# K pairs one place later, their tokens spread over three w2 pairs, phi of the third segment's K moved there, and the mixing product in one step

## The chip, the cores and the metric

The kernel runs on one core of a Trainium2 chip. The metric is the device time of one execution in microseconds; the profile's span (first to last instruction) is about 1.7 to 2 us shorter.

Names: TensorE (PE, weight loads PEld), VectorE (DVE), ScalarE (ACT), GpSimd (POOL), SyncE (SP). SyncE does nothing here but issue DMAs, in program order, waiting for each one's semaphores.

## The reference, cut to what matters

```python
xn = layernorm(x)                                  # x: 2048 tokens x 1024
# B: token MLP with weights w1 (2048 x 3584) and w2 (3584 x 2048)
# A: attention, 32 heads of 32, in 4 segments of 512 tokens, with a memory M, z over segments
q, k, v = xn @ wq, xn @ wk, xn @ wv
phi = lambda t: where(t > 0, t + 1, exp(t))
for s in range(4):
    a_dot = softmax(qs @ ks.T * scale + mask) @ vs
    a_mem = (phi(qs) @ M) / (phi(qs) @ z + 1e-6)
    outs.append(g * a_mem + (1 - g) * a_dot)       # the "mixing"
    M, z = M + phi(ks).T @ vs, z + sum(phi(ks))
return x + concat(outs) @ wo + B(layernorm(xn))
```

phi of K is needed for three segments only: the memory after the fourth is not used.

## The kernel before: the parts that the change and the argument touch

The MLP's products are done by a seven-product scheme (Winograd's form of Strassen's): a *pair* of 128-column blocks takes 7 products, in the order 1, 6, 5, 7, 2, 4, 3. A w2 pair has 7 x 14 matmuls, and there are 8 of them, here counted 0 to 7. Between them stand 4 *K pairs* (7 x 4 matmuls each), which compute K of segments 3 and 4 and store it in DRAM. After the w2 stage comes attention: 32 *units* (8 per segment, counted 0 to 31); a unit's time runs from its first exponential on ScalarE to the next unit's.

```python
    N_KP, K_FIRST = N_GRP // 2, 3                  # order: w2 0 1 2, K, 3, K, 4, K, 5, K, 6 7

    def k_prepare(self, i, p):                     # after product p of w2 pair i
        n = self.ORDER.index(p)
        if i < 2:                                  # 8 blocks of tokens (128 each) of segments 3, 4
            c = 8 + 4 * i
            if n in (2, 3, 4, 5):
                m = n - 2
                self.xn_scale(c + m, F16)          # VectorE
                ...                                # DMA transpose xnK <- xs, on SyncE
            if n < 4:
                self.xn_load(c + n)                # two buffers xs: waits for the transpose that reads it
        g = i - self.K_FIRST + 1
        if g == 0 and n < 4:                       # pair 2: the four differences of the K scheme
            self.differences(self.kB, self.R_kB, self.kD, self.R_kD, (n + 1,))
        ...
    def after2(self, pair, p):                     # cut
        elif p == 4:
            finish("Y", 1, 0, t1)
            self.put_out(...)
            if i + 2 < self.N_W2:
                self.load_w2(i + 2)                # 1.79 MB on SyncE's queue
        ...
        self.k_prepare(i, p)
        if i >= self.N_W2 - 2:                     # pairs 6 and 7: two of attention's first tokens each
            c = 2 * (i - self.N_W2 + 2)
            if p in (1, 6):
                self.xn_load(c + (p == 6))
            elif p in (5, 7):
                self.xn_scale(c + (p == 7))
                self.xn_transpose(c + (p == 7))
        if i == self.N_W2 - 1:
            self.before_attention(p)               # after 1: wq, wk; after 6: wv (2 MB); after 2: wo (2 MB)
```

In a unit of attention, TensorE's matmuls are cut into stretches; at certain stops one entry of a list of *side work* is taken, which is mostly VectorE's:

```python
            self.jobs.extend(self.unit_jobs(u))    # unit_jobs also issues the k load of unit u + 2
            if xn:
                self.xn_load(c)                    # a token of the next segment
            ...
                steps = self.combine(u - 1)        # [scales, products(0), products(1), add]
                self.side.append(steps.pop(0))
            if N_GRP <= u:
                self.side.append(lambda u=u: self.phi_q(u))
            if u:
                self.side.extend(steps)
            if u + 1 < N_UNIT:
                self.side.append(lambda u=u: (self.phi_k(u + 1), self.k_transpose(u + 1)))
            if xn:
                self.side.append(lambda c=c: (self.xn_scale(c), self.xn_transpose(c)))
```

## Time and profile before

| | us |
|---|---|
| time, median of 3 | 676.55 (675.97 to 676.81) |
| span of the profiled run | 673.8 |
| w2 pair 1 / 2 / the undisturbed ones | 22.7 / 30.3 / 21.15 |
| first K pair / the other three | 7.9 / 6.24 |
| units 16 to 22, even / odd | 9.78 / 7.1 to 7.6 |
| unit 24 (no phi of K) | 8.89 |

From the page of the kernel before, TensorE's line of section 1 (busy us, share, count) and the granted clock in 40 slices:

```profile
PE 643.2 (95%) x4559; PEld 301.9 (45%) x4610; DVE 449.6 (67%) x853; ACT 281.1 (42%) x305; POOL 147.3 (22%) x181
...
PEclk9999999999999979999999999999999999999999
```

TensorE is nearly always busy, so only its gaps and its one clock dip can be won. The table of windows of the kernel before, cut at w2 pairs 1 and 2, the first K pair, pair 3, pair 7 and units 16 to 23 (length, then busy time and count for each engine, granted clock, DMA share, GB/s):

```profile
core 0: us, PE busy (x) PEld busy (x) DVE busy (x) ACT busy (x) POOL busy (x), PEclk, DMA share, GB/s
201.04:223.72 22.68, 21.32 (x100) 9.50 (x99) 9.07 (x12) 0.60 (x1) 4.23 (x3) 1.00 0.84 212
223.72:253.97 30.25, 23.14 (x99) 9.90 (x98) 16.20 (x20) 0.60 (x1) 4.23 (x3) 0.89 0.51 129
253.97:261.85 7.88, 6.31 (x29) 2.57 (x28) 6.30 (x10) 1.19 (x2) 0.00 (x0) 1.00 0.95 245
261.85:283.00 21.15, 21.15 (x99) 9.60 (x98) 8.98 (x14) 0.60 (x1) 4.23 (x3) 1.00 0.33 105
365.17:386.54 21.37, 21.32 (x99) 9.66 (x99) 7.18 (x14) 2.11 (x3) 4.60 (x6) 1.00 0.99 252
530.10:597.80 67.70, 61.75 (x694) 30.95 (x705) 63.83 (x133) 53.32 (x52) 26.96 (x33) 1.00 0.59 141
```

Pair 2 has the same 98 matmuls as pair 3 and takes 9.1 us more, with a clock of 0.89. In the last line VectorE is busy 63.8 of 67.7 us, TensorE 61.8: VectorE is the bound there. The timeline of the kernel before shows what happened in pair 2 (start, duration, engine, what; in brackets the idle time before it and what ended it):

```profile
227.60 0.45 SPq L220 DMA_DIRECT2D w2s<-in_B_w_dram  x1
228.71 6.70 SPq L220 DMA_TRANSPOSE xnK<-xs  x1
...
238.17 1.23 DVE L664 TENSOR_TENSOR kD<-xnK,xnK 128x2048 f16<-128x2048 f16 x1 [7.84 <-issue]
...
240.06 5.01 PE L198 MATMUL ps_all<-g,sum 128*128 128x512 f16 x14 [7.11 <-DVE part L690]
```

A token's transpose normally keeps SyncE 1.23 us and lands about 3 us after its issue. This one stood behind a w2 load of 1.79 MB: 6.70 us of issue, landed at 237.9. VectorE stood before the first K difference until then, and TensorE 7.1 us behind VectorE; then 14 matmuls took 5.0 us instead of 3.2, at half clock. In attention the chain of work that ended last runs through VectorE (start, us, what; the view leaves the shortest pieces out):

```profile
536.09 0.69 DVE pqT L1183
536.79 1.05 DVE prod L1413
537.86 1.01 DVE prod L1413
539.24 0.73 DVE mtmp L1181
540.00 1.00 DVE mtmp L1183
```

### The profile page before, as it was taken

Reading aid. Unit: us, or ns where it says so; the run is one execution under the profiler, and the core shown is the slowest. Engines: PE = TensorE matmul, PEld = TensorE weight load, DVE = VectorE, ACT = ScalarE, POOL = GpSimd, SP = SyncE. Lnnn points to the kernel's source line nnn. Section 1 sums busy time; section 2 is a strip of 40 time slices with the busy share of each in tenths; the row PEclk is TensorE's granted clock in tenths of the full one; section 3 lists DMA queues with packets and bytes.
Section 4 is the critical chain, followed back from the end, with each engine's and each line's share of the span. In section 5 each row is a group of like instructions: output and inputs, shape, how many; then the busy total and the mean of one; then the engine's idle time right before and its main releaser. Section 6 shows DMA issues by size and latency. Waiting matters only on the chain.

```text
span 673.8 us, 11152 instructions
## 1 busy us (share of the span) xinstructions
PE 643.2 (95%) x4559; PEld 301.9 (45%) x4610; DVE 449.6 (67%) x853; ACT 281.1 (42%) x305; POOL 147.3 (22%) x181
## 2 busy tenths in 40 slices
PE   8999999999999879999999999999999998999987
PEld 3444444444444333444444444455444444444444
DVE  6965766656652565627445326756998999997895
ACT  7532322313200001000011047778767877788860
POOL 2500000000020120201202203433233433444340
PEclk9999999999999979999999999999999999999999
DMA  8704332422959828256183966755665467444425
GB/s 309 192 1 125 85 102 63 125 64 63 241 156 252 195 62 234 67 167 182 52 248 93 275 184 165 155 120 117 144 147 103 126 163 166 112 104 111 117 59 133
DMA packets 188972, 93.96 MB, mean 139 GB/s; under 512 B 108536, under 2 KB 175096, under 8 KB 188920
## 3 DMA queue, kind: packets, MB, share of 16 engines
q1 hardware_dynamic: 188776, 93.20, 53.7%
q8 instruction: 36, 0.59, 0.4%
q14 instruction: 16, 0.13, 0.1%
q10 hardware_dynamic: 144, 0.03, 0.0%
HBM read 69.23 MB, written 10.49 MB: 118 GB/s over the span
## 4 chain that ended last, share of the span: by engine, by line
PE 48%; DVE 12%; issue 3%; ACT 1%; DMA 1%; DVEq 0%
PE ps_all L198 48%; DVE prod L1413 3%; DVE ost L1366 2%; DVE pqT L1183 1%; ACT pT L1315 1%; DVE mtmp L1181 1%; DVE fin L1258 1%; DVE mtmp L1183 1%; DVE srec L1408 1%; DMA oT<-o_s 1%; DVE fin L1559 1%; DVE MZbf L1376 0%; DVE srec L1409 0%; DVE xs L1087 0%; DVE sum L649 0%
## 5 line engine op out<-in xcount | busy, mean ns | idle before, releaser
L1315 ACT ACTIVATE pT<-ps_all 128x2048 bf16<-128x2048 f32 x80 | 150.1, 1876 | 49.9 <-PE ps_all L198 49.7
L1319 POOL TENSOR_SCALAR_AFFINE_SELECT pT<-pT 128x512 bf16<-128x512 bf16 x128 | 98.2, 784 | 175.9 <-ACT pT L1315 175.9
L690 DVE TENSOR_TENSOR part<-ps_all,part 128x512 f32<-128x512 f32 x84 | 58.0, 691 | 109.7 <-PE ps_all L198 108.9
L1025 POOL TENSOR_TENSOR part<-part,stg 128x512 f32<-128x512 f32 x24 | 33.2, 1409 | 301.6 <-DVE part L690 301.6
L695 ACT ACTIVATE part<-ps_all 128x512 f32<-128x512 f32 x24 | 14.3, 597 | 168.1 <-PE ps_all L198 168.1
L746 ACT ACTIVATE g<-part,b1c 128x512 f16<-128x512 f32 x36 | 26.0, 722 | 98.7 <-DVE part L690 98.7
L198 PE MATMUL ps_all<-wv,xnT 128*128 128x512 bf16 x241 | 63.3, 380 | 1.4 <-DVE kT L1213 0.8
L198 PE MATMUL ps_all<-wo,oT 128*128 128x512 bf16 (+2 forms) x257 | 62.7, 366 | 1.2 <-DMA oT<-o_s 0.3
L198 PE MATMUL ps_all<-xnT,wq 128*128 128x512 bf16 x241 | 60.6, 379 | 1.3 <-issue 1.1
L198 PE MATMUL ps_all<-g,sum 128*128 128x512 f16 x224 | 52.8, 389 | 7.1 <-DVE part L690 7.1
L198 PEld LDWEIGHTS ps_all<-vA,pT 128*128 128x128 bf16 x1280 | 45.0, 96 | 27.9 <-DVE ost L1366 13.4
L1366 DVE CAST ost<-ps_all 128x396 bf16<-128x396 f32 (+2 forms) x96 | 43.4, 472 | 18.3 <-PE ps_all L198 17.7
L198 PE MATMUL ps_all<-vA,pT 128*128 128x33 bf16 x1280 | 48.6, 178 | 6.0 <-DVE ost L1366 6.0
L198 PE MATMUL ps_all<-g,w2s 128*128 128x512 f16 x224 | 51.0, 379 | 0.0
L198 PE MATMUL ps_all<-gT,sum 128*128 128x512 f16 x224 | 49.7, 379 | 0.0
L1413 DVE TENSOR_TENSOR prod<-ost,srec 128x512 bf16<-128x512 bf16 x48 | 45.9, 956 | 0.8
L198 PE MATMUL ps_all<-h,sum 128*128 128x512 f16 x192 | 45.2, 379 | 0.0
L198 PE MATMUL ps_all<-h,w1s 128*128 128x512 f16 x192 | 44.9, 379 | 0.0
L198 PE MATMUL ps_all<-hT,sum 128*128 128x512 f16 x192 | 43.6, 379 | 0.0
L198 PEld LDWEIGHTS ps_all<-g,sum 128*128 128x128 f16 x224 | 22.2, 100 | 35.2 <-DVE part L690 7.6
L198 PE MATMUL ps_all<-qT,kT 32*128 32x384 bf16 (+3 forms) x512 | 31.7, 301 | 3.8 <-ACT pT L1315 1.9
L198 PEld LDWEIGHTS ps_all<-xnT,wq 128*128 128x128 bf16 x256 | 22.9, 97 | 27.3 <-issue 4.4
(115 smaller groups left out, 850.6 us busy)
## 6 DMA issues: line engine op xcount, KB each, us to landing
w2s<-in_B_w_dram SPq DMA_DIRECT2D x8, 1792.0 KB, 8.7
w1s<-in_B_w_dram SPq DMA_DIRECT2D x12, 1024.0 KB, 5.4
wq<-in_A_wq_dram SPq DMA_DIRECT2D x32, 256.0 KB, 3.2
xs<-in_A_x_dram SPq DMA_DIRECT2D x24, 256.0 KB, 3.5
stg<-in_A_x_dram SPq DMA_DIRECT2D x16, 256.0 KB, 4.1
out_dram<-stg SPq DMA_DIRECT2D x16, 256.0 KB, 3.1
wk<-in_A_wk_dram SPq DMA_DIRECT2D x16, 256.0 KB, 3.5
fin<-out_dram SPq DMA_DIRECT2D x16, 256.0 KB, 3.4
```

The costliest lines, as they stand in the source:

```text
L198: ins = self.nc.tensor.matmul(*args, **kwargs)
L690: self.fw.op("dve", lambda e: e.tensor_tensor(self.tmp[dst][:], self.bank(b), self.tmp[src][:], op=ALU.add), reads=[self.R_bank[b], self.R ...
L695: self.fw.op("act", lambda e: e.activation(self.tmp[dst][:], self.bank(b), ACT.Copy), reads=[self.R_bank[b]], writes=[self.R_tmp[dst]])
L746: self.fw.op("act", lambda e: e.activation(self.gB[f % 2][half][:, f // 2, :], src, ACT.Gelu_apprx_tanh, bias=self.b1c[:, f:f + 1], scale= ...
L1025: fw.op("pool", lambda e: e.tensor_tensor(self.tmp[t][:], self.tmp[t][:], self.stg[k][:, 512 * half:512 * half + 512], op=ALU.add), reads= ...
L1181: fw.op("dve", lambda e: e.tensor_scalar(mt[:], et[:], 1.0, None, op0=ALU.min), reads=[R_et], writes=[self.R_mtmp[k]])
L1183: fw.op("dve", lambda e: e.scalar_tensor_tensor(dst, src, 1.0, mt[:], op0=ALU.add, op1=ALU.max), reads=[R_src, self.R_mtmp[k]], writes=[R_ ...
L1258: self.fw.op("dve", lambda e: e.tensor_tensor(dst, self.bank(b), dst.bitcast(F16), op=ALU.add), reads=[self.R_bank[b], R], writes=[R])
L1315: fw.op("act", lambda e: e.activation(dst, src, ACT.Exp, scale=SCALE), reads=self.R_bank[0:4], writes=[R[v % 2][kb] for v, kb, _ in blocks ...
L1319: fw.op("pool", lambda e: e.affine_select(d, d, pattern=[[0, 4], [1, P]], compare_op=ALU.is_ge, fill=0.0, base=0, channel_multiplier=-1), ...
L1366: fw.op("dve", lambda e: e.tensor_copy(dst, src), reads=[self.R_bank[b]], writes=[self.R_ost[o][part]])
L1413: fw.op("dve", lambda e: e.tensor_tensor(self.prod[:, n, :], ost[:, n, 0:D_HEAD], rec[:, n].unsqueeze(2).to_broadcast([P, 16, D_HEAD]), op ...
```

## The change: its intent, and the diff

Three intents: the eight tokens of the K pairs get more time each, and the K differences a pair more (K pairs one place later, tokens over pairs 0 to 2); VectorE loses work in units 16 to 22 (phi of the third segment's K is computed in the K pairs, stored in DRAM and read back by a transposing DMA); and it runs one product of 1024 columns instead of two of 512. K pairs later also means that the memory of attention's first tokens is free only in pair 7, so all four tokens go there.

```diff
-    N_KP, K_FIRST = N_GRP // 2, 3
+    N_KP, K_FIRST = N_GRP // 2, 4
@@ after_k: put(acc, row, col, t)
-            fw.dma(self.k_d[v], dst[:], reads=[R], writes=[self.R_kd[v]], is_output=True)
+            if (row, col) in ((0, 1), (1, 0)):        # both columns of a row in one store
+                ...
+            if col == 0:
+                n = t1 if row else t3
+                e, R_e = self.tmp[n][:].bitcast(BF16)[:, 0:SEG_L], self.R_tmp[n]
+                fw.op("act", lambda q: q.activation(e, dst, ACT.Exp), ...)
+                fw.op("dve", lambda q: q.tensor_scalar(e, e, 1.0, None, op0=ALU.min), ...)
+                fw.op("dve", lambda q: q.scalar_tensor_tensor(e, dst, 1.0, e, op0=ALU.add, op1=ALU.max), ...)
+                fw.dma(self.pk_d[v], e, reads=[R_e], writes=[self.R_pkd[v]], is_output=True)
@@ k_prepare(i, p)
-        n = self.ORDER.index(p)
-        if i < 2: ...
+        n = 7 * i + self.ORDER.index(p)
+        if n % 2 == 0 and 2 <= n // 2 < 10:           # a token at every second product
+            m = n // 2 - 2
+            c = 8 + m
+            self.xn_scale(c, F16)
+            self.fw.dma(self.xnK[m // 4][...], self.xs[c % 2][:].bitcast(F16), ..., transpose=True, own=True)
+        if n % 2 == 0 and n // 2 < 8:
+            self.xn_load(8 + n // 2)
+        n %= 7
         ...
+        if i == self.N_W2 - 1:                        # attention's first four tokens, all in pair 7
+            if 1 <= n < 5:
+                self.xn_scale(n - 1)
+                self.xn_transpose(n - 1)
+            if n < 3:
+                for c in ((0, 1), (2,), (3,))[n]:
+                    self.xn_load(c)
@@ after2
-        if i >= self.N_W2 - 2: ...                    # two tokens in pair 6, two in pair 7
@@ k_transpose(u)
+        if 0 <= v < N_GRP:
+            self.fw.dma(self.pk[j][:], self.pk_d[v], reads=[self.R_pkd[v]], writes=[self.R_pk[j]], transpose=True)
@@ combine(u)
-        return [scales, lambda: products(0), lambda: products(1), add]
+        return [scales, products, add]
```

More of the change, by code (lines that the diff above doesn't have):

```diff
@@ L903, in kout @@
         def kout(w, k):
-            t, (r,) = w.take(f"kout{k}", [P, SEG_L], BF16)
+            t, r = w.take(f"kout{k}", [P, 2, SEG_L], BF16, 2)
             self.kout.append(t)
@@ L908, in alloc_w2_rest @@
         kout(w, 0)
+        w = _Walk(self.mem, self.B_AT + self.K_AT, self.B_AT + self.FREE_AT)
         kout(w, 1)
-        w = _Walk(self.mem, self.B_AT + self.K_AT, self.B_AT + self.FREE_AT)
-        kout(w, 2)
-        kout(w, 3)
         self.xs, self.R_xs = [], []
@@ L936, in alloc_w2_rest @@
         self.R_kd = [Res(f"kd{u}") for u in range(N_UNIT // 2)]
+        self.pk_d = self.nc.dram_tensor("pk_part", (N_GRP, P, SEG_L), BF16).ap()
+        self.R_pkd = [Res(f"pkd{u}") for u in range(N_GRP)]
         self.load_wkp(0)
@@ L966, in put @@
         def put(acc, row, col, t):
-            n, b = 2 * row + col, pair.bank[acc]
-            dst, R = self.kout[n], self.R_kout[n]
+            b = pair.bank[acc]
+            dst, R = self.kout[row][:, col, :], self.R_kout[row][col]
             if t is None:
-                fw.op("act", lambda e: e.activation(dst[:], self.bank(b), ACT.Copy), reads=[self.R_bank[b]], writes=[R])
+                fw.op("act", lambda e: e.activation(dst, self.bank(b), ACT.Copy), reads=[self.R_bank[b]], writes=[R])
             else:
-                fw.op("dve", lambda e: e.tensor_tensor(dst[:], self.bank(b), self.tmp[t][:], op=ALU.add),
+                fw.op("dve", lambda e: e.tensor_tensor(dst, self.bank(b), self.tmp[t][:], op=ALU.add),
                       reads=[self.R_bank[b], self.R_tmp[t]], writes=[R])
             v = N_GRP * col + 2 * g + row
-            fw.dma(self.k_d[v], dst[:], reads=[R], writes=[self.R_kd[v]], is_output=True)
+            if (row, col) in ((0, 1), (1, 0)):
+                v = 2 * g + row
+                fw.dma(self.k_d.rearrange("(c v) p t -> v p c t", c=2)[v], self.kout[row][:], reads=self.R_kout[row],
+                       writes=[self.R_kd[v], self.R_kd[v + N_GRP]], is_output=True)
+            if col == 0:
+                n = t1 if row else t3
+                e, R_e = self.tmp[n][:].bitcast(BF16)[:, 0:SEG_L], self.R_tmp[n]
+                fw.op("act", lambda q: q.activation(e, dst, ACT.Exp), reads=[R], writes=[R_e])
+                fw.op("dve", lambda q: q.tensor_scalar(e, e, 1.0, None, op0=ALU.min), reads=[R_e], writes=[R_e])
+                fw.op("dve", lambda q: q.scalar_tensor_tensor(e, dst, 1.0, e, op0=ALU.add, op1=ALU.max),
+                      reads=[R, R_e], writes=[R_e])
+                fw.dma(self.pk_d[v], e, reads=[R_e], writes=[self.R_pkd[v]], is_output=True)
         if p == 1:
@@ L995, in k_prepare @@
     def k_prepare(self, i, p):
-        n = self.ORDER.index(p)
-        if i < 2:
-            c = 8 + 4 * i
-            if n in (2, 3, 4, 5):
-                m = n - 2
-                self.xn_scale(c + m, F16)
-                s, cc = (c + m) // 4, m
-                x = self.xs[m % 2]
-                self.fw.dma(self.xnK[s - 2][:, :, cc * P:(cc + 1) * P], x[:].bitcast(F16), reads=[self.R_xs[m % 2]],
-                            writes=[self.R_xnK[s - 2][cc]], transpose=True, own=True)
-            if n < 4:
-                self.xn_load(c + n)
+        n = 7 * i + self.ORDER.index(p)
[3 more added lines that the diff above has]
+            self.xn_scale(c, F16)
+            self.fw.dma(self.xnK[m // 4][:, :, (m % 4) * P:(m % 4 + 1) * P], self.xs[c % 2][:].bitcast(F16),
+                        reads=[self.R_xs[c % 2]], writes=[self.R_xnK[m // 4][m % 4]], transpose=True, own=True)
+        if n % 2 == 0 and n // 2 < 8:
+            self.xn_load(8 + n // 2)
+        n %= 7
         g = i - self.K_FIRST + 1
@@ L1068, in after2 @@
         self.k_prepare(i, p)
-        if i >= self.N_W2 - 2:
-            c = 2 * (i - self.N_W2 + 2)
-            if p in (1, 6):
-                self.xn_load(c + (p == 6))
-            elif p in (5, 7):
-                self.xn_scale(c + (p == 7))
-                self.xn_transpose(c + (p == 7))
         if i == self.N_W2 - 1:
@@ L1191, in phi_k @@
     def phi_k(self, u):
-        if u // N_GRP < N_SEG - 1:
+        if u < N_UNIT // 2:
             k = u % 3
@@ L1196, in k_transpose @@
     def k_transpose(self, u):
-        if u // N_GRP < N_SEG - 1:
-            j = u % 2
+        j, v = u % 2, u - N_UNIT // 2
+        if 0 <= v < N_GRP:
+            self.fw.dma(self.pk[j][:], self.pk_d[v], reads=[self.R_pkd[v]], writes=[self.R_pk[j]], transpose=True)
+        elif v < 0:
             self.fw.dma(self.pk[j][:], self.mtmp[1][:], reads=[self.R_mtmp[1]], writes=[self.R_pk[j]], transpose=True)
@@ L1409, in scales, with products @@
             fw.op("dve", lambda e: e.tensor_tensor(rv, rv, g8, op=ALU.mult), reads=[R_rec, self.R_gate], writes=[R_rec])
-        def products(half):
-            n = slice(16 * half, 16 * half + 16)
-            fw.op("dve", lambda e: e.tensor_tensor(self.prod[:, n, :], ost[:, n, 0:D_HEAD],
-                                                   rec[:, n].unsqueeze(2).to_broadcast([P, 16, D_HEAD]), op=ALU.mult),
-                  reads=R_ost + [R_rec, self.R_prod], writes=[self.R_prod])
+        def products():
+            fw.op("dve", lambda e: e.tensor_tensor(self.prod[:], ost[:, :, 0:D_HEAD],
+                                                   rec.unsqueeze(2).to_broadcast([P, 32, D_HEAD]), op=ALU.mult),
+                  reads=R_ost + [R_rec], writes=[self.R_prod])
         def add():
@@ L1524, in attention @@
             self.dense(100)
-            if N_UNIT // 2 <= u + 2 < 3 * N_GRP:
-                self.exps.append((1, self.kT[(u + 2) % 3], self.R_kT[(u + 2) % 3], u + 2))
         while self.side:
```

## The prediction

> **What bounds it now.** TensorE is busy 95% of the 673.8 us span, so only its gaps can be won. From the timeline and the table of windows:
> - w2 stage, 180-386 us. A pair takes 21.1 us undisturbed. Pair 1 took 22.7 us (a 1.35 us gap), pair 2 30.2 us: TensorE idle 7.1 us at 233-240, then granted clock 0.53 (240-244 us), so 14 matmuls took 5.0 us, not 3.2. The first K pair took 7.9 us, the second 6.2. Loss about 12 us. Cause: the fourth and eighth token transposes were issued about 1 us after a 1.79 MB w2 load and held the SyncE queue 7.2 and 6.7 us; VectorE waited for the tokens (7.8 us before the first K difference), TensorE for VectorE.
> - Attention. Units 16-22 have VectorE idle 0.3-0.7 us each and TensorE idle 0.5-1.0 us; the even ones take 9.78 us against 8.9 in unit 24, which lacks phi of K. VectorE bounds there (63.1 us busy of 530-597). Loss about 5.5 us; units 10, 11, 26, 30 and the end have about 2-3 us more.
>
> **What the change does.**
> 1. Tokens at every second product over three pairs, differences a whole pair later. Two transposes still follow a w2 load, but there are 12 us per token instead of about 3. Walking the queue by hand leaves about 1 us of stall. Gain 11 us.
> 2. Phi of segment 3's K leaves attention: 8 x (VectorE 0.29 to 0.72 + 0.69 to 1.0 us, ScalarE 0.62). In the K pairs (about 2 us VectorE each) it follows the additions TensorE waits for: free.
> 3. One 1024-column product for two of 512 (677 ns alone, 1.0-1.1 us beside GpSimd). The fixed part is about 0.14 us (677 ns less 512 columns at 0.96 GHz): 1.3-1.9 us instead of 1.7-2.2.
>    2 and 3 make units 16-22 TensorE-bound: gain 5-7 us with the small gaps.
> 4. The cost: all four tokens for attention now fall in the last w2 pair, after the last K pair. SyncE order there: wq, wk, transpose 0, load 2 (waits for transpose 0), wv (2 MB), transpose 1, load 3 (waits for transpose 1), transposes 2, 3. Before, the transpose behind wv landed 10.3 us after wv's issue. So: wv at +11 to +15 us of the pair, transpose 1 lands +21 to +25, load 3 2.9 us, scaling 0.6, transpose 3 3.1: the first q projection starts at +28 to +32 instead of +21.3. Loss 7-11 us, plus about 1.5 us of lowered clock, as at 240 us (Trainium skill, "TensorE: Matmul & The Clock Gate", "What's actually happening": half rate after an idle window of about 3.4 us; this trace agrees, 0.53).
>
> **Sum:** 676.5 - 11 - 6 + 9 = 668 us. Range 659 to 676. Faster by over 2% 0.20, within 2% 0.77, slower 0.03.
>
> **What would show it.** (1) No gap or clock dip near 235 us; pairs 1 and 2 at 21-22.5 us. (2) Units 16-22 even about 8.9, odd about 6.6 us, VectorE idle 1.5 us or more; transposes of phi from DRAM landing in 2-5 us, unwaited for. (3) 24 products of about 1.2-1.7 us. (4) A TensorE gap of 7-10 us just before the first wq matmul, VectorE waiting for the fourth token's load.
>
> **What would make it wrong.** If wv does not hold back transpose 1, item 4 shrinks: 658-662. If the w2 stage stalls again behind the two transposes after w2 loads, 3-6 us come back.

## The result, and the profile after

The changed kernel takes 677.81 us (677.60 to 678.37, 4 runs), the kernel before 676.26 us (674.73 to 676.81, 4 runs). The ratio is 1.0028, with a 95% interval of 1.001 to 1.0046. So: no gain, a loss of a quarter of a per cent, and 1.8 us beyond the upper end of the predicted range.

The page after:

```profile
PE 650.6 (96%) x4610; PEld 303.2 (45%) x4610; DVE 442.4 (65%) x829; ACT 282.0 (42%) x305; POOL 155.8 (23%) x181
...
PEclk9999999999999989999999889999999999999999
```

There are two clock dips now, a shallower one at the old place and a new one around 385 us. The windows of the changed kernel, for the same stages (w2 pairs 1, 2, 3, the first K pair, pair 7 with what follows until the first wq matmul, from there to unit 0, units 16 to 23), and then two stretches for their clock:

```profile
200.62:221.77 21.15, 21.15 (x99) 9.57 (x98) 10.69 (x13) 0.60 (x1) 4.23 (x3) 1.00 0.81 202
221.77:247.10 25.33, 23.01 (x100) 9.95 (x98) 10.69 (x14) 0.60 (x1) 4.23 (x3) 0.93 0.88 189
247.10:268.25 21.15, 21.15 (x99) 9.60 (x98) 13.49 (x15) 0.60 (x1) 4.23 (x3) 1.00 0.54 145
268.25:276.13 7.88, 6.31 (x29) 2.58 (x28) 5.65 (x9) 2.19 (x3) 0.00 (x0) 1.00 0.96 242
358.30:388.92 30.62, 21.31 (x100) 9.54 (x99) 10.56 (x24) 1.34 (x3) 4.43 (x6) 0.92 0.84 201
388.92:405.85 16.93, 16.93 (x69) 6.95 (x70) 2.02 (x4) 4.22 (x7) 0.00 (x0) 0.84 0.67 200
535.40:600.10 64.70, 62.26 (x706) 31.43 (x705) 53.76 (x109) 49.72 (x46) 28.72 (x33) 1.00 0.63 144
...
384.00:394.00 10.00, 5.08 (x13) 1.76 (x14) 2.35 (x8) 0.60 (x1) 0.00 (x0) 0.50 0.88 239
240.70:244.00 3.30, 3.30 (x9) 1.22 (x8) 3.30 (x4) 0.00 (x0) 2.90 (x2) 0.50 0.91 263
```

VectorE has 10 us less to do in units 16 to 23 (53.8 against 63.8), and the stage became only 3.0 us shorter. Put side by side, the profiled runs account for the whole difference of the spans (673.8 to 676.3):

| stage, in us | before | after | difference |
|---|---|---|---|
| w2 pair 1 | 22.68 | 21.15 | -1.5 |
| w2 pair 2 | 30.25 | 25.33 | -4.9 |
| first K pair | 7.88 | 7.88 | 0 |
| start of pair 7 to the first wq matmul | 21.37 | 30.62 | +9.2 |
| first wq matmul to unit 0 | 14.14 | 16.93 | +2.8 |
| units 8 to 15 | 70.39 | 70.46 | +0.1 |
| units 16 to 23 | 67.71 | 64.70 | -3.0 |
| unit 24 to the end | 75.95 | 76.21 | +0.3 |
| the rest | | | -0.4 |
| span | 673.8 | 676.3 | +2.5 |

The timeline of the changed kernel in pair 2, at the end of pair 7, and in unit 18:

```profile
224.17 0.44 SPq L220 DMA_DIRECT2D w2s<-in_B_w_dram  x1
224.65 8.15 SPq L220 DMA_TRANSPOSE xnK<-xs  x1
...
238.16 0.55 DVE L1096 TENSOR_SCALAR xs<-xs,ln_mv,ln_rs 128x1024 f16<-128x1024 bf16 x1 [9.45 <-DMA xs<-in_A_x_dram]
...
239.36 4.88 PE L198 MATMUL ps_all<-gT,w2s 128*128 128x512 f16 x14 [2.32 <-DVE part L690]
...
388.92 3.57 PE L198 MATMUL ps_all<-xnT,wq 128*128 128x512 bf16 x8 [9.31 <-DMA xnT<-xs]
...
554.71 0.57 PE L198 MATMUL ps_all<-vA,pT 128*128 128x33 bf16 x16 [1.47 <-DVE ost L1377]
```

A transpose behind a w2 load again: 8.15 us of issue. This time the next token's load waits for it (two buffers), and VectorE waits 9.45 us for that load. TensorE loses 2.3 us, and 1.9 us more at half clock (4.2 us together, 25.33 less 21.15). The chain of work that ended last runs through DMAs at the two places that matter:

```profile
367.00 5.04 DMA xnT<-xs
372.06 1.49 DMA xs<-in_A_x_dram
373.55 8.53 DMA xnT<-xs
382.10 2.79 DMA xs<-in_A_x_dram
384.94 0.43 issue
385.37 0.11 DVE stg L1049
385.48 3.19 DMA xnT<-xs
...
549.94 3.67 DMA xs<-in_A_x_dram
553.67 0.43 issue
554.09 0.57 DVE ost L1377
```

At 372.45 the 2 MB of wv went into the queue; the second transpose, issued at 373.55, needed 8.53 us to land. The load of the fourth token had to wait for it, and the fourth transpose for that load. At 549.94 the load of an attention token was issued so late that VectorE, which now is early, stood waiting for it, and TensorE behind VectorE (1.5 us in unit 18, 1.0 us in unit 20).

The Trainium skill's page "DMA: Bandwidth & Descriptors", section "Queues, rings and completion order", says that each DMA engine takes the descriptors of one queue's ring in order. That agrees with what is seen here: the 256 KB transpose behind the w2 load on the same queue landed only just after it (the load of w2 at 224.17 landed at 234.45, the transpose behind it at 235.29). For wv the trace has no landing time.

### The profile page after: what moved, and what is told of

The parts are those of the page before. It is cut to its first block, busy times and chain, and to the rows that moved or that the text cites. A ratio compares the mean times of both kernels' runs of the same rounds, so it can differ in the third digit from the quotient of the medians. Undisturbed runs are those within 1.5% of the kernel's fastest.

```text
span 676.3 us, 11182 instructions
## 1 busy us (share of the span) xinstructions
PE 650.6 (96%) x4610; PEld 303.2 (45%) x4610; DVE 442.4 (65%) x829; ACT 282.0 (42%) x305; POOL 155.8 (23%) x181
## 4 chain that ended last, share of the span: by engine, by line
PE 83%; DMA 7%; DVE 5%; issue 1%; ACT 1%; SPq 1%; POOL 0%; DVEq 0%
PE ps_all L198 83%; DMA xnT<-xs 2%; DMA xs<-in_A_x_dram 2%; DMA xnK<-xs 2%; ACT pT L1326 1%; SPq L220 1%; DVE ost L1377 1%; DVE prod L1423 1%; DMA oT<-o_s 1%; DMA xin<-in_A_x_dram 1%; DVE fin L1567 1%; DVE fin L1269 0%; DVE mtmp L1190 0%; DVE o_s L1429 0%; DVE srec L1419 0%
## 5 line engine op out<-in xcount | busy, mean ns | idle before, releaser
L1330 POOL TENSOR_SCALAR_AFFINE_SELECT pT<-pT 128x512 bf16<-128x512 bf16 x128 | 107.2, 855 | 176.7 <-ACT pT L1326 176.7
L198 PE MATMUL ps_all<-xnT,wq 128*128 128x512 bf16 x256 | 66.1, 387 | 9.3 <-DMA xnT<-xs 9.3
L198 PE MATMUL ps_all<-wv,xnT 128*128 128x512 bf16 x256 | 67.7, 380 | 0.0
L198 PE MATMUL ps_all<-wo,oT 128*128 128x512 bf16 (+2 forms) x272 | 66.1, 367 | 0.7 <-DMA oT<-o_s 0.5
L198 PEld LDWEIGHTS ps_all<-vA,pT 128*128 128x128 bf16 x1280 | 45.5, 96 | 25.3 <-DVE ost L1377 7.9
L198 PE MATMUL ps_all<-g,sum 128*128 128x512 f16 x224 | 51.0, 379 | 0.0
L198 PEld LDWEIGHTS ps_all<-xnT,wq 128*128 128x128 bf16 x256 | 23.2, 99 | 37.8 <-issue 15.9
L1423 DVE TENSOR_TENSOR prod<-ost,srec 128x1024 bf16<-128x1024 bf16 x24 | 36.4, 1515 | 0.0
L198 PEld LDWEIGHTS ps_all<-wo,oT 128*128 128x128 bf16 x272 | 23.2, 97 | 25.8 <-issue 6.1
```

Of the source, the lines that this page charges most:

```text
L198: ins = self.nc.tensor.matmul(*args, **kwargs)
L1330: fw.op("pool", lambda e: e.affine_select(d, d, pattern=[[0, 4], [1, P]], compare_op=ALU.is_ge, fill=0.0, base=0, channel_multiplier=-1), ...
L1423: fw.op("dve", lambda e: e.tensor_tensor(self.prod[:], ost[:, :, 0:D_HEAD], rec.unsqueeze(2).to_broadcast([P, 32, D_HEAD]), op=ALU.mult), ...
```

## The experiments

The theory after the result: four separate losses, each a wait for a small DMA or for VectorE order. (a) The tokens of attention stand behind wv. (b) The fifth token of the K pairs stands behind a w2 load. (c) VectorE, freed of phi, reaches attention's tokens before their loads have landed. (d) The first K pair's 1.57 us gap belongs to VectorE's order in the pair ahead of it, not to the token stall. Each has a rival, given with the expectations.

| run | median us | ratio to before (95%) |
|---|---|---|
| changed kernel | 677.81 | 1.0028 (1.001 to 1.0046) |
| e1: wv after the tokens | 669.63 | 0.9905 (0.9877 to 0.9933) |
| e2: w2 load after the token | 673.92 | 0.9965 (0.9933 to 0.9998) |
| e3: attention's token load first | 675.63 | 0.9995 (0.9973 to 1.0016) |
| e4: schedule undone | 674.10 | 0.9965 (0.9934 to 0.9996) |
| e5: one-step product alone | 674.03 | 0.9979 (0.9956 to 1.0002) |
| e6: differences early | 675.51 | 0.9991 (0.996 to 1.0021) |
| e7: three mends | 660.14 | 0.9769 (0.975 to 0.9788) |
| e8: four mends | 659.58 | 0.9762 (0.9743 to 0.9782) |
| e9: four mends, two products | 657.48 | 0.9732 (0.9714 to 0.975) |
| e10: e8 once more | 659.32 | 0.9758 (0.974 to 0.9776) |
| e11: one product and an empty entry | 657.15 | 0.9728 (0.9714 to 0.9742) |
| e12: e9 once more | 657.16 | 0.9731 (0.9717 to 0.9744) |

All were correct.

### e1: wv after the tokens

```diff
         if p == 6:
             self.wv, self.R_wv = take("wv", ...)
-            for bv in range(2):
-                fw.dma(self.wv[:, :, bv * 512:(bv + 1) * 512], ...)
@@
         elif p == 2:
             self.wo, (self.R_wo,) = take("wo", ...)
+            for bv in range(2):
+                fw.dma(self.wv[:, :, bv * 512:(bv + 1) * 512], ...)
```

> The changed kernel with the wv load issued after the fourth attention token's transpose instead of before the second's. Theory (the transposes wait behind wv's 2 MB): transposes land within 3.5 us of issue, the gap before the first wq matmul falls from 9.3 us to at most 3.5 us, the clock dip shortens; time falls by 7 to 10 us, to about 668 to 671 us. Rival (four tokens through two buffers do not fit in one pair, whatever is ahead of them in the queue): the gap stays at 6 us or more and the time falls by less than 4 us.

Lines of e1's timeline:

```profile
371.14 1.23 SPq L220 DMA_TRANSPOSE xnT<-xs  x1
...
379.06 1.25 SPq L220 DMA_DIRECT2D wv<-in_A_wv_dram  x2
...
381.39 1.89 PE L198 MATMUL ps_all<-xnT,wq 128*128 128x512 bf16 x8 [3.02 <-DMA xnT<-xs]
```

The second transpose, 4.87 us of issue in the changed kernel, takes 1.23 us again, and the gap falls from 9.31 to 3.02 us without any half clock behind it. The ratio falls from 1.0028 to 0.9905, about 8.3 us of 676. In the profiled runs the stretch from the start of pair 7 to unit 0 is 8.05 us shorter (24.33 and 15.17 us, against 30.62 and 16.93). Two other differences have nothing to do with the edit: pair 2's gap was not followed by half clock (23.2 us instead of 25.3), and unit 18's was (12.4 us instead of 10.5); the last section returns to this. Theory (a) holds. The rest of the gap, 3 us, is the rival's share: load, scale, transpose, twice through two buffers.

### e2: w2 load after the token

```diff
-            if i + 2 < self.N_W2:                # in p == 4, ahead of k_prepare
-                self.load_w2(i + 2)
         ...
         self.k_prepare(i, p)
+        if p == 4 and i + 2 < self.N_W2:
+            self.load_w2(i + 2)
```

> The changed kernel with each w2 load issued after that product's token transpose, not before it. Theory: the 8 us issue of the fifth token's transpose falls to about 1.3 us, the VectorE wait of 9.5 us for the seventh token goes, third pair of w2 falls from 25.3 to 21.2 us, first K pair stays at 7.9 us; time falls by 3.5 to 4.5 us to about 673.5 us. Rival (two token buffers alone make the chain too slow): third pair stays over 23.5 us.

The windows of e2, pair 2:

```profile
222.05:243.21 21.16, 21.16 (x100) 9.60 (x99) 10.74 (x14) 0.60 (x1) 3.38 (x3) 1.00 0.86 215
```

Pair 2 takes 21.16 us, as an undisturbed one, and the first K pair stays at 7.88. The time fell to 673.92 us (673.5 expected). Theory (b) holds; two buffers are enough if no large load stands ahead of a transpose.

### e3: attention's token load first

```diff
+            if xn:
+                self.xn_load(c)
             self.jobs.extend(self.unit_jobs(u))  # with the k load
-            if xn:
-                self.xn_load(c)
```

> The changed kernel with each attention token's load issued at the head of its unit, before that unit's k load, whose wait holds the queue. Theory (VectorE, freed of phi, now reaches the token's scaling before the load has landed): the TensorE gaps of 1.5 and 1.0 us in units 18 and 20 go, the third segment falls from 64.7 to about 62.5 us, time falls by 2 to 3 us to about 675.3 us. Rival (the transposes of phi from DRAM hold the queue, or the longer product against GpSimd): the gaps stay, time within 0.7 us of the changed kernel.

The windows of e3, units 16 to 23:

```profile
535.30:598.00 62.70, 62.47 (x706) 31.37 (x705) 53.51 (x109) 49.77 (x45) 28.71 (x33) 1.00 0.63 149
```

62.7 us instead of 64.7, and the gaps of units 18 and 20 are gone although phi is still read from DRAM. Those transposes land after 2.8 us in the median and nobody waits for them. The ratio is 0.9995 against 1.0028, about 2.2 us; the two intervals overlap, so the 2.0 us of the traces is the firmer figure. A small shift is enough: unit 18's load is issued at 548.68 instead of 549.94 and lands at 552.23 instead of 553.60, and VectorE scales the token at 552.25. That the k load's *wait* holds the queue, as the expectation has it, is not seen: the k load takes 0.64 us of issue there. Theory (c) holds. Whether VectorE is early because phi is gone or because the list of side work is shorter, e3 does not separate; e5 below, with the shorter list and phi kept, has no wait for a token in these units.

### e4 and e5: parts of the change alone

e4 is the kernel before with phi moved and the one-step product, but with the K pairs and tokens at their old places (in the diff of the change, the parts of `K_FIRST`, `k_prepare` and `after2` are left out). e5 is the kernel before with the one-step product alone (only the last hunk).

> The kernel before with only the arithmetic parts of the change: phi of the third segment's K in the K pairs, read back transposed, and the one-step mixing product; K pairs and tokens at their old places. Theory: the attention part is as in the changed kernel (u0 to end about 270.4 us against 273.1), the w2 stage as in the kernel before, the start of attention as before: about 673.6 us, 0.4% faster than before. Rival (the phi work in the K pairs costs TensorE time there): K pairs over 6.3 us each and the time no better than before.

> The kernel before with only the one-step mixing product. The change takes 9.5 us of VectorE busy time in 24 products. Theory (units 16 to 22 were bound by VectorE, and both parts relieve it): even units 16 to 22 fall from 9.78 to about 9.2 to 9.5 us, odd ones stay near 7, the third segment falls from 67.7 to about 66 us; time about 675 us, less than half of the arithmetic parts' gain without the token stalls. Rival (the product alone frees enough of VectorE and phi adds nothing): third segment at 65 us or less.

e4: 674.10 us, from unit 0 to the end 271.7 us (270.4 expected, 273.1 before). The K pairs take 6.24 us, as before, so phi is free there. The shortfall is unit 18: a gap of 1.75 us waiting for a token, with half clock behind it, 12.5 us instead of 8.9. e5: 674.03 us, 1.7 us under the kernel before in its rounds, though 1.5 us of the profiled run's advantage is pair 1, where the small gap happened not to occur. Its third segment is 66.65 us; even units are 9.6 to 10.4 us. So the product alone does not free enough, and phi's move is the larger part (e9 below, with phi's move and two products, brings this stage to 61.9 us). As times, e4 and e5 are alike, and the interval of e5 just includes 1: this rests on the stages of the traces. e5 also has the shorter list that e11 below is about; the product with a list of the old length was not run on the kernel before.

### e6: the differences early

```diff
-        if g == 0 and n < 4:
-            self.differences(self.kB, self.R_kB, self.kD, self.R_kD, (n + 1,))
+        if g == 0 and n < 2:
+            self.differences(self.kB, self.R_kB, self.kD, self.R_kD, (2 * n + 1, 2 * n + 2))
```

> The changed kernel with the four K differences made after the first two products of the pair ahead of the first K pair, not after its first four. Theory (the first K pair's 1.57 us gap comes of VectorE being late with the last two differences and the sums behind them): first K pair 6.24 us as the others instead of 7.88, time about 1.6 us less, about 675.5 us. Rival (the gap belongs to a first K pair, whatever VectorE does, or stems from the token schedule): it stays at 7.9 us.

The windows of e6, first K pair:

```profile
267.02:273.26 6.24, 6.24 (x30) 2.56 (x29) 4.00 (x6) 2.19 (x3) 0.00 (x0) 1.00 1.14 284
```

The gap is gone, and 675.51 us is what was expected; but the ratio's interval overlaps that of the changed kernel, and in this profiled run too pair 2 was free of half clock, so it is the trace that shows it. Theory (d) holds: the prediction had counted this 1.6 us as a consequence of the token stall, and it was not.

### e7 and e8: the mends together

e7 has the edits of e2 and e3 and a new order for attention's first tokens; e8 adds e6's.

```diff
-        if i == self.N_W2 - 1:
-            if 1 <= n < 5: ...
-            if n < 3: ...
+        if i == self.N_W2 - 2 and n == 6:        # end of pair 6: the first two loads
+            self.xn_load(0)
+            self.xn_load(1)
+        if i == self.N_W2 - 1 and n < 2:         # after pair 7's first two products, ahead of wq, wk and wv
+            for c in (2 * n, 2 * n + 1):
+                self.xn_scale(c)
+                self.xn_transpose(c)
+            if n == 0:
+                self.xn_load(2)
+                self.xn_load(3)
```

(The third and fourth transposes still come behind wq and wk, 1 MB together, but ahead of wv.)

> The changed kernel with w2 loads after token transposes, attention's token loads at the head of their units, and the four first tokens loaded from the end of the pair before, scaled and transposed after the last pair's first two products, ahead of wq, wk and wv. Theory: the losses add: third w2 pair 21.2 us, no gap over 1 us and no half clock before the first wq matmul, third segment about 62.7 us; 677.8 less 4.2, less 12, less 2.7 gives about 659 us. Rival (loads now late elsewhere, wv for the first v product or wq for unit 2): a new gap of 2 us or more at the start of attention, 662 us or more.

> The kernel of the three mends with the K differences after the first two products as well. Theory: another 1.6 us less than it, about 657.5 us, over 2% faster than before. Rival: the same time as the three mends.

The windows of e7, pair 7 and from the first wq matmul to unit 0:

```profile
354.36:375.51 21.15, 21.15 (x100) 9.59 (x98) 9.32 (x18) 1.35 (x3) 4.42 (x6) 1.00 0.89 205
375.51:389.86 14.35, 14.35 (x70) 6.36 (x69) 3.25 (x10) 4.22 (x7) 0.00 (x0) 1.00 1.14 317
```

No gap, no half clock. 660.14 us (659 expected): the losses add. e8 takes 659.58 us. Its first K pair is 6.23 us as expected, but only 0.6 us of the 1.6 arrives in the time (1.1 us in the span): in its profiled run the w2 stage began 0.5 us later than in e7's, and attention took 0.3 us more, which nothing in the edit explains.

### e9 to e12: is the one-step product worth anything?

In every run with the one-step product, unit 10 had a gap of 1.1 us that the kernel before does not have (0.4 there). e9 is e8 with two products again. e10 is e8 again, for the same rounds.

> The kernel of the four mends with the mixing product in two steps again, so only phi's move is left of the arithmetic parts. Theory (phi's move frees VectorE by about 1 us a unit, the product by about 0.4 us, and either alone leaves units 16 to 22 near the TensorE bound): third segment within 1 us of 62.8 us; the new 1.1 us gap of unit 10, seen in every run with the one-step product, goes back to 0.4 us; time within 1.5 us of the four mends. Rival (the one-step product carries the gain of units 16 to 22): third segment 64.5 us or more, time 2 us or more above the four mends.

> The kernel of the four mends once more, in the same rounds, for the comparison with two steps: 659 to 660.5 us, 0.976 of the kernel before.

The mended kernel is 1.8 us *faster* with two products (657.48 against 659.32), although VectorE is then busier: the theory had allowed for 1.5 us either way, not for this. Its other two forecasts held: the third segment takes 61.9 us, and unit 10's gap is back at 0.4 us. There are two differences: the product's length, and that the list of side work is one entry longer, so what follows in it is taken a stop later. e11 tells them apart by keeping one product and putting an empty entry where the second was:

```diff
-        return [scales, products, add]
+        return [scales, products, lambda: None, add]
```

> The kernel of the four mends with the one-step product and an entry that does nothing in the list of side work, where the second product stood, so that all other side work comes at the stops it had with two products. Theory A (the one-step product costs time because the list is one entry shorter and the token's scaling, phi and k copies come a stop earlier, before their inputs): time falls from 659.3 to 657.5 us or less, third segment 62 us, unit 10 back to 11.8 us. Theory B (it is the long product itself: 1.65 us beside GpSimd[...]): time stays at 659 us or more, unit 10 at 12.5 us.

> The kernel of the four mends with two products once more, in the same rounds: 657.2 to 657.8 us, 0.973 of the kernel before.

e11: 657.15 us, e12: 657.16 us. Theory A holds. Lines of VectorE's timeline at the start of unit 19, of e10:

```profile
541.10 0.73 DVE L1432 TENSOR_TENSOR o_s<-prod 128x512 bf16<-128x512 bf16 x1
543.73 0.55 DVE L1099 TENSOR_SCALAR xs<-xs,ln_mv,ln_rs 128x1024 bf16<-128x1024 bf16 x1 [1.90 <-DMA xs<-in_A_x_dram]
```

and of e11, with its window of units 16 to 23 (a line of the table of windows) in the second fence:

```profile
540.46 0.73 DVE L1432 TENSOR_TENSOR o_s<-prod 128x512 bf16<-128x512 bf16 x1
541.12 0.85 DVE L1099 TENSOR_SCALAR xs<-xs,ln_mv,ln_rs 128x1024 bf16<-128x1024 bf16 x1
```

```profile
517.00:579.00 62.00, 62.00 (x706) 31.61 (x705) 54.86 (x109) 49.80 (x45) 27.58 (x33) 1.00 0.65 153
```

SyncE's queue shows how the shorter list made the load late: in e10 the token before is scaled a stop earlier, so its transpose (issued at 537.22) stands ahead of this token's load (540.03, landed at 543.71); in e11 the load goes first (536.91, landed at 540.95) and that transpose follows (538.99). With the empty entry VectorE does not wait for the token, TensorE is busy all 62.0 us of the stage, and unit 10 falls from 12.49 to 11.56 us. So the one-step product does no harm itself. It frees little (the 24 products take 36.4 us together instead of 45.9 for 48, but the addition behind them takes 0.74 us in the median instead of 0.43), and once phi is gone TensorE, not VectorE, is the bound, so the freed time is worth nothing there. (In units 8 to 15, which keep phi, e11 is 1.0 us shorter than e12 in the profiled runs, 69.4 against 70.4; the medians of the whole do not show it.) What cost time was the shorter list.

The best versions, e11 and e12, take 0.973 of the time of the kernel before.

## Why the prediction was wrong

The mechanisms that the prediction named did act; three terms of its sum were mis-sized, the second because of waits that it did not name, and all in one direction: 4.5, 3.3 and 3.0 us in the profiled runs, together a little more than the 9.8 us by which 668 missed 677.8.

1. **"Gain 11 us" in the w2 stage: 6.5 us (1.5 in pair 1, 4.9 in pair 2).** The step that failed is "walking the queue by hand leaves about 1 us of stall". The prediction saw that two transposes would follow a w2 load. It took the 12 us per token to absorb that; pair 2 lost 4.2 us instead (2.3 us of gap, the rest at half clock). The prediction's last paragraph had named this case as what would make it wrong ("3-6 us come back"), but the sum did not count it. e2 shows it: without the load ahead, 21.16 us. The half-clock part is not certain: in e1 and e6 the same stall (1.85 and 1.93 us) had none behind it, and pair 2 took about 23.2 us. In addition the first K pair's 1.6 us was put into the gain; e6 shows that it has another cause, VectorE's order.
2. **"2 and 3 ... gain 5-7 us with the small gaps": 2.7 us.** Units 16 to 22 did become TensorE-bound where nothing else stood in the way (8.89 and 6.59 us, as predicted). The step that failed is the assumption that nothing else waits: VectorE now reached the token's scaling before the load had landed (1.5 and 1.0 us of gap, e3), and the shorter list of side work moved what follows a stop earlier, a token's transpose ahead of the next token's load among it (e11). With both mended, unit 0 to the end takes 266.4 us in e11 against 273.1 before: 6.7 us, the size that was predicted. The last sentence of item 2, that phi is free in the K pairs, held: 6.24 us.
3. **"Loss 7-11 us, plus about 1.5 us of lowered clock": 9.2 plus 2.8 us.** The first q projection was predicted at +28 to +32 us of pair 7 and started at +30.6, VectorE waiting for the fourth token's load as the prediction said. Only the clock term was too small: in pair 2 of the kernel before, TensorE lost about 1.8 us of matmul time after its gap; here the clock was halved from 384 to 394 us, and TensorE was at work for the second half of that. That the half clock follows a long gap is what the Trainium skill's page "TensorE: Matmul & The Clock Gate", section "What's actually happening", says, and the windows show 0.50.

So the loss was foreseen and the gains were taken at full size, as if nothing else could be waiting behind the wait that was removed. The one-step product's own estimate (1.3 to 1.9 us) was nearly right: 1.22 us for the one of the 24 that overlapped no GpSimd mask, 1.65 in the median. Its fixed part of about 0.14 us comes out as well: twice the shortest 512-column product (677 ns) less the shortest of 1024 columns (1217 ns). The Trainium skill's page "SBUF — State Buffer", section "Who interferes with whom", gives a reason that fits: a two-input VectorE operation and a GpSimd one that reads SBUF exclude each other. In the trace of before, 43 of 48 products overlapped GpSimd's mask and took 0.99 us in the mean, the 5 others 0.69. The mechanism itself was not tested by a run here.

## What to carry to other kernels

On an in-order DMA queue ask, for each small transfer that something waits for, what large load is issued just ahead of it; moving the load behind it, at no cost seen here, was worth 4 us in one place and 8 in another. When an engine is relieved, it reaches its next inputs sooner: check that their loads move forward too, and that a list of work handed out at fixed stops keeps its length. A gain and a loss of a change can hide each other, so undo or mend the parts one by one before discarding it: here 1.003 became 0.973.

## What the Trainium skill lacked or had wrong

- Page "TensorE: Matmul & The Clock Gate": half rate comes, it says, after at least one idle window of about 3.4 us. Here a gap of 1.67 us in unit 18 of e1 was followed by 3.4 us at a granted clock of 0.50, and one of 2.32 us in the changed kernel likewise, while gaps of 1.85 and 3.02 us in e1 were not followed by any. So a gap well under the window can be enough, and one near it need not be. Where the gap falls seems to decide, and a window need not be idle throughout: the traces' clock records fit stretches of 3.41 us on a fixed grid (the changed kernel's two drops, at 240.57 and 383.94, are 42.0 of them apart, and lowered clock lasted 3.41, 6.83 or 10.24 us). Counted within one such stretch, idle times of 2.09 us (e3) and 2.20 us (changed kernel) in pair 2 were followed by half clock, and 1.93 us (pair 2 of e6) and 1.92 us (the larger part of e1's 3.02) were not; in unit 18, with its smaller matmuls, 1.67 us (e1) and 1.75 us (e4) were. No run was made to test this, and which share of idle time is needed in which stage stays open.
- Page "DMA: Bandwidth & Descriptors": it describes ring order, but gives no figure for a transpose behind a large load on the same queue. Here its issue alone took 4.9 to 8.2 us instead of 1.2, and SyncE issued nothing else meanwhile (in the kernel before, its next DMA after the transpose of 228.71 came at 235.47).
- The same page gives a bandwidth for transposes, but no landing time of one small one: 128 KB took 2.5 us from SBUF (kernel before) and 2.8 us from DRAM (changed kernel; medians, issue to landing).
- Page "SBUF — State Buffer": of a VectorE operation that overlaps GpSimd it quotes two measured slowdowns without operation or size; here a 128 x 1024 product took 1.22 us when it overlapped no mask and 1.65 in the median (23 of 24 overlapped one).
